# Turning ten column blocks of a weight by DMA in the opening instead of on TensorE between two forward passes

## The chip, the core and the metric

The kernel runs on one core of a Trainium2 chip. Its time is the device time of that core in microseconds (us), from the first to the last instruction and what lies around them; less is better. The times given for it are 2131.66, 2133.43 and 2137.64 us (median 2133.43). The profile is of one more execution.

## The reference, cut to what matters

Four layers, A, B, A, B, each added to the residual stream x (2048 rows of 640, bf16), and the gradients of x and of the four weights. Both layers share the form layer norm, Wqkv, attention over 32 heads of 20, Wo. A is a linear attention, B a softmax attention over a window of 256 rows.

```python
def _A_ref(x, wqkv, wo):
    qkv = ((x @ wqkv).reshape(B, S, 3, H, Dh)).transpose(2, 0, 3, 1, 4)
    q, k, v = qkv[0], qkv[1], qkv[2]
    phi = lambda t: jnp.where(t > 0, t + 1, jnp.exp(t)) + 1e-6
    pq, pk = phi(q), phi(k)
    kv = jnp.einsum("bhsd,bhse->bhde", pk, v)
    z = jnp.einsum("bhsd->bhd", pk)
    num = jnp.einsum("bhqd,bhde->bhqe", pq, kv)
    den = jnp.einsum("bhqd,bhd->bhq", pq, z)[..., None] + 1e-6
    o = num / den
    return o.transpose(0, 2, 1, 3).reshape(B, S, D) @ wo
...
def reference(A_x, A_wqkv, A_wo, B_wqkv, B_wo, B_x, grad_out):
    _const = dict(B_x=B_x)
    def _f(*_d):
        return _fwd_reference(**{'A_x': _d[0], 'A_wqkv': _d[1], 'A_wo': _d[2], 'B_wqkv': _d[3], 'B_wo': _d[4], **_const})
    _out, _vjp = jax.vjp(_f, A_x, A_wqkv, A_wo, B_wqkv, B_wo)
    _grads = _vjp(grad_out)
    _out0 = jnp.asarray(_out)
    return (_out0, *[jnp.asarray(_g) for _g in _grads])
```

The gradient of a product with a weight needs the weight turned (its columns as rows): dx = dy @ W^T. Each weight is turned once, kept in DRAM (WqTA, WoTA, WoTB, WqTB), and read back in the backward phases.

## The kernel before

The 2048 rows are 16 tiles of 128. The forward part has these stretches:

- **The opening** (`a_first(items, 0, 0)`): layer norm of each tile, its transposes on TensorE, Wqkv of the first layer A in six chunks of 320 columns (`a_qkv`), the exponentials on ScalarE, the rest on VectorE. Each tile stores hn (its normed rows, on SP's queue) and pq, pk and v (on ScalarE's queue). The ring of hn has one buffer, so the layer norm of a tile waits until the hn store of the tile before has landed.
- **The first double pass** (`a_kv(0)`, `ab_pass(0, False)`): the sums over the rows of layer A (`a_kv`; L572 are the last "band sums"), then for each tile A's numerator (`a_num`), its projection (`out_proj`), layer B, and the third layer's layer norm and Wqkv.
- **Between the passes** and **the second double pass** (`late_q`, `a_kv(2)`, `turn_w` twice, `ab_pass(2, True)`): the same for layers three and four. The q columns of the third layer are made later (`late_q`, L547), eight tiles of them between the passes.

The backward part follows, phase by phase, with orders of its own. It reads the turned weights back from DRAM long after they were written.

The weights are turned in two ways. `flip_w` lets the DMA turn a block of 128 by 640 of a weight in DRAM into a buffer of the ring KT or e (five and four buffers, which the attention uses later), and stores it to DRAM; it makes twenty flips in the opening, fifteen for B's Wqkv and five for A's Wo, each flip and each store on SP's queue. `turn_w` turns 128 columns with five transposes on TensorE (L906), copies them from PSUM to SBUF on ScalarE (L911), and stores them over SP; it makes the fifteen column blocks of A's Wqkv and the five of B's Wo between the passes. Its three PSUM buffers are the ring `sb`, so every fourth turn waits for the copy of the first. The copies of Wo_B go over the space of v and wait for the last user of it. Operations of `turn_w` and of eight tiles of `late_q` are marked as fillers.

The order of each engine in the forward part comes from a list scheduler, `Sched.order`: it takes the operation that can start first by the durations written with each operation, and a filler counts as starting 300 ns later than it could. A flip or a store of `flip_w` has the kind "B": SP is taken for 1.3 us, and it ends 4.5 us after its start. The items of a stretch are written down in order of a number in tiles (`items`), and a flip additionally waits for the layer norm of a tile (`gate`). Once emitted, each engine works its list in order. SP's and ScalarE's DMAs are counted by eight completion counters that are taken in turn in the order of emission; a DMA waits until the last one of its counter, the eighth before it, has landed.

The lines that the change touches:

```python
for i in range(4 * DT):                       # DT = 5: twenty flips
    at = 4.5 + 0.5 * i
    items.append((at, len(items), flip_w(i, ("rs", 0, int(at) - 1))))
...
turn_w("Wqkv_A", self.QTT, ...)               # QTT = 15 column blocks
turn_w("Wo_B", DT, ...)
```

Of the kernel before, what the change touches and what calls it, by code (L numbers as in the profile page):

```python
# [16 lines left out]
P = 128  # L17
# [69 lines left out]
class Sched:  # L87
# [6 lines left out]
    def op(self, eng, dur, fn, r=(), w=(), dma=None, prio=None, filler=False):  # L94

        o = Op()
        o.filler = filler
        o.eng, o.dur, o.fn, o.dma, o.idx = eng, dur, fn, dma, len(self.ops)
        o.prio = o.idx if prio is None else prio
        o.deps, o.after, o.users, o.bufs, o.est, o.end = set(), set(), [], [], 0.0, None  # L100
        o.start = None
        for k in r:
            if k in self.lw:
                o.deps.add(self.lw[k])
            self.rd.setdefault(k, []).append(o)
        for k in w:
            if k in self.lw:
                o.deps.add(self.lw[k])
            o.deps.update(self.rd.pop(k, ()))
            self.lw[k] = o  # L110
        o.deps.discard(o)
        for k in list(r) + list(w):
            b = k[0] if isinstance(k, tuple) else k
            if isinstance(b, Buf) and b not in o.bufs:
                o.bufs.append(b)
                if b.ops:
                    o.after.add(b.ops[0])
                elif b.idx:
                    o.after.add(b.pool.items[b.idx - 1].ops[0])
                if not b.ops and b.idx >= b.pool.n:  # L120
                    o.deps.update(b.pool.items[b.idx - b.pool.n].ops)
                b.ops.append(o)
        self.ops.append(o)
        return o
# [78 lines left out]
class Kern:  # L203
# [129 lines left out]
    def forward(self, slabs):  # L333
        nc, tc, D, T, TT, DT, H, G, DP = self.nc, self.tc, self.D, self.T, self.TT, self.DT, self.H, self.G, self.DP
# [4 lines left out]
        with ExitStack() as st:  # L339
# [26 lines left out]
            at = [0]  # L366
# [14 lines left out]
            def over_vv(n):  # L381
                vat[0] += n
                assert vat[0] <= TT * D
                return vflat[:, vat[0] - n:vat[0]]
            WoTB = over_vv(DT * D).rearrange("p (k n) -> p k n", k=DT)
# [26 lines left out]
            def dma(eng, out, in_, size, r, w, **kw):  # L412
                def f():
                    with nc.allow_non_contiguous_dma(reason="strided layouts"):
                        dq[eng].dma_start(out=out(), in_=in_())
                op(eng, 60, f, r, w, dma=("D", size), **kw)

            def flip(out, in_, size, r, w, **kw):
                op("SP", 60, lambda: nc.sync.dma_start_transpose(out=out(), in_=in_()), r, w, dma=("T", size), **kw)

            def pe(cols):
                return sum(max(c / 2.4 + 3, 26) for c in cols)

            def av(n):
                return 170 + 0.834 * n
# [463 lines left out]
            def run(items):  # L889
                for _, _, f in sorted(items, key=lambda it: it[:2]):  # L890
                    f()

            def load_w(name, src, eng, k, after=()):
                v = src.rearrange("(kt p) n -> p kt n", p=P)
                dma(eng, lambda: wsb[name][:, k:k + 1, :], lambda: v[:, k:k + 1, :], 2 * P * wsb[name].shape[-1], after, [name])

            def turn_w(name, n, keys, dst, done, after=()):

                F = dict(filler=True)
                for q in range(n):  # L900
                    ps = R["sb"].buf()
                    ps.make = lambda ps=ps: singles[ps.idx % 3].bitcast(BF).rearrange("p (k q) -> p k q", q=P)

                    def f(ps=ps, q=q):
                        for et in range(DT):
                            nc.tensor.transpose(ps.t[:, et, :], wsb[name][:, et, q * P:(q + 1) * P], self.ident)  # L906
                    o = op("PE", pe([P] * DT), f, keys, [ps], **F)
                    o.deps.update(o_ for o_ in R["s3"].items[-1].ops if not o_.filler)
                    turned.append(o)
                    out, key = dst(q)  # L910
                    turned.append(op("ACT", av(D), lambda ps=ps, out=out: nc.scalar.copy(out(), ps.t[:, 0:DT, :]), [ps],  # L911
                                     [key], **F))
                    turned[-1].deps.update(after)
                    turned[-1].deps.discard(turned[-1])
                    done(q, out, key)

            def flip_w(i, gate):
                def f():
                    et, part = divmod(i, 4)
                    src, name, n, a = ((self.B_wqkv, "WqTB", self.QTT, part * DT) if part < 3 else (self.A_wo, "WoTA", DT, 0))  # L920
                    c0 = part * D if part < 3 else 0
                    kind = ("KT", "e")[i % 2]
                    b = R[kind].buf()
                    view = lambda: (b.t if kind == "KT" else b.t.rearrange("p h i q -> p (h i) q"))[:, 0:DT, :]
                    flip(view, lambda: src[et * P:(et + 1) * P, c0:c0 + D], 160 * KB, [gate], [b])
                    S.ops[-1].dma = ("B", 0)
                    dma("SP", lambda: W[name].rearrange("p (a b) -> p a b", a=n)[:, a:a + DT, et * P:(et + 1) * P],
                        view, 160 * KB, [b], [])
                    S.ops[-1].dma = ("B", 0)
                return f  # L930
# [4 lines left out]
            def staged(W_, n):  # L935
                def dst(q):
                    kind = ("KT", "e")[len(turned) // 2 % 2]
                    b = R[kind].buf()
                    return (lambda: b.t[:, 0:DT, :] if kind == "KT" else
                            b.t.rearrange("p h i q -> p (h i) q")[:, 0:DT, :]), b  # L940

                def done(q, out, b):
                    dma("SP", lambda: W[W_].rearrange("p (a b) -> p a b", a=n)[:, q, :].rearrange("p (k q) -> p k q", q=P),
                        out, 160 * KB, [b], [])
                return dst, done
# [103 lines left out]
            items = []  # L1049
# [4 lines left out]
            for i, (k, src) in enumerate((("Wo_A", self.A_wo), ("Wqkv_B", self.B_wqkv), ("Wo_B", self.B_wo))):  # L1054
                for j in range(DT):
                    tt = 1 + 3 * i + j
                    items.append((tt + 0.9, len(items), lambda k=k, src=src, j=j, tt=tt: load_w(k, src, "SP", j, [("vv", tt, 5)])))
            for i in range(4 * DT):
                at = 4.5 + 0.5 * i
                items.append((at, len(items), flip_w(i, ("rs", 0, int(at) - 1))))  # L1060
            run(items)
            a_kv(0)
            ab_pass(0, False)
            for tt in range(EARLY):
                late_q(2, tt, filler=True)
            a_kv(2)
            kv_users = {o for t in range(TT) for k in [("pk", t, 2), ("pk", t, 3), ("vv", t, 4), ("vv", t, 5)]
                        for o in S.rd.get(k, ())}
            turn_w("Wqkv_A", self.QTT, [("Wqkv_A", i) for i in range(6)], *staged("WqTA", self.QTT))
            turn_w("Wo_B", DT, ["Wo_B"], lambda q: (lambda: WoTB[:, q, :].rearrange("p (k q) -> p k q", q=P), ("WoTB", q)),  # L1070
                   lambda q, out, key: None, kv_users)
            R["s3"].items[-1].ops.extend(turned)
            a_users = {o for i in range(6) for o in S.rd.get(("Wqkv_A", i), ())}
# [3 lines left out]
            for rows, kind, size, f in slabs:  # L1077
                keys = [("dOp", t) for t in rows] or [("qkvp", 3, t, i) for t in range(TT) for i in (1, 3, 5)]
# [810 lines left out]
```

## Time and profile before

| | us or share |
|---|---|
| median of three runs | 2133.43 |
| the profiled execution | 2123.76 |
| its span, first to last instruction | 2122.0 |
| TensorE busy | 94% |
| VectorE, ScalarE, GpSimd busy | 69%, 57%, 41% |
| mean granted TensorE clock | 0.981 |
| opening | about 10 to 105 us |
| turns of the weights on TensorE | 386 to 434 us |
| end of the second double pass | about 700 us |

Rows of instructions in order of time read: start, duration, engine, line, operation, tile written and tiles read, and how many are merged in the row. A bracket gives the idle time of the engine ahead of it and what ended that. PE is TensorE, ACT ScalarE, DVE VectorE, POOL GpSimd. SPq and ACTq are the DMA issues of SP and ScalarE; their duration is the time that the issue held the queue, not that of the transfer, which is given as "DMA to landing". Rows of a line read: minimum, median and maximum of the duration in ns, and the first and last start in us.

### The profile page before, as it was taken

The numbers are of one execution on the slowest core, as the hardware profiler recorded it, in microseconds if no ns is written. First come the engines' busy times: TensorE is split into PE (matmuls) and PEld (weight loads), VectorE is DVE, ScalarE is ACT, GpSimd is POOL, SyncE is SP. The second block draws the span as 40 slices with busy tenths as digits, with TensorE's granted clock in tenths as the row PEclk, the third lists the DMA queues.
The fourth block names the chain that finished last, engine by engine and source line by source line (L and its number), as shares of the span: only waits on it lengthen the run. The fifth ranks groups of instructions, "written<-read, shape, count | busy, mean of one in ns | idle before, by whom it ended". The sixth has DMA issues, their size and how long they took to land. (4 is left out here: it accounts for less than half of the span.)

```text
span 2122.0 us, 67891 instructions
## 1 busy us (share of the span) xinstructions
PE 2003.0 (94%) x27908; PEld 1384.9 (65%) x27908; DVE 1456.4 (69%) x3018; ACT 1204.6 (57%) x1995; POOL 878.8 (41%) x1850
## 2 busy tenths in 40 slices
PE   7979999889999899999999899999999999998999
PEld 4746666666666676776666677556777765666764
DVE  7767887677775688999544389407999984445751
ACT  4628888557887588888322133217898881211430
POOL 1026666137777465665232123204666651321210
PEclk9999999999999999999999999998999999999999
DMA  9838988479989688998888999746999989979853
GB/s 283 211 102 185 186 186 179 128 190 198 194 204 184 129 153 153 156 156 169 180 186 184 207 202 210 147 119 132 162 156 160 155 172 177 201 177 228 181 112 101
DMA packets 934471, 365.94 MB, mean 172 GB/s; under 512 B 820752, under 2 KB 914448, under 8 KB 933904
## 3 DMA queue, kind: packets, MB, share of 16 engines
q1 hardware_dynamic: 866176, 299.16, 72.6%
q10 hardware_dynamic: 67984, 62.45, 9.6%
q8 instruction: 218, 3.57, 0.7%
q14 instruction: 93, 0.76, 0.1%
HBM read 109.02 MB, written 101.58 MB: 99 GB/s over the span
## 5 line engine op out<-in xcount | busy, mean ns | idle before, releaser
L1689 DVE TENSOR_TENSOR ds_sb<-pair,e_sb 128x768 bf16<-128x768 f32 x480 | 437.8, 951 | 58.0 <-PE pair L1650 48.6
L1669 ACT ACTIVATE e_sb<-pair 128x768 bf16<-128x768 f32 x480 | 390.8, 815 | 97.2 <-PE pair L1650 68.1
L832 POOL TENSOR_SCALAR_AFFINE_SELECT e_sb<-e_sb 128x384 bf16<-128x384 bf16 (+1 forms) x512 | 197.2, 406 | 334.5 <-ACT e_sb L823 328.0
L823 ACT ACTIVATE e_sb<-s_ps 128x1152 bf16<-128x1152 f32 (+2 forms) x256 | 273.9, 1070 | 93.4 <-PE s_ps L819 66.3
L1681 POOL TENSOR_SCALAR_AFFINE_SELECT e_sb<-e_sb 128x256 bf16<-128x256 bf16 x448 | 182.0, 406 | 228.1 <-ACT e_sb L1669 227.9
L1320 POOL TENSOR_TENSOR gw<-w,gcar 128x640 f32<-128x640 f32 x64 | 89.4, 1397 | 423.3 <-ACT w L1317 402.2
L1131 PEld LDWEIGHTS <-slabR 128*128 128x128 bf16 x1920 | 185.8, 98 | 116.8 <-DMA slabR<-o 6.2
L1678 POOL TENSOR_SCALAR_AFFINE_SELECT e_sb<-e_sb 128x256 bf16<-128x256 bf16 x512 | 206.5, 406 | 90.1 <-ACT e_sb L1669 90.1
L1714 PEld LDWEIGHTS <-dsT 128*128 128x128 bf16 x2880 | 146.4, 97 | 99.0 <-issue 91.8
L1705 ACT COPY dsT<-dsT_ps 128x768 bf16<-128x768 bf16 x240 | 191.2, 796 | 9.5 <-PE dsT_ps L1702 6.6
L447 PE MATMUL mm_ps<-slabR,hnTB 128*128 128x320 bf16 x960 | 166.8, 301 | 4.4 <-DVE oA L647 2.4
L1702 PE MATMUL dsT_ps<-ident,ds_sb 128*128 128x128 bf16 x1848 | 158.9, 224 | 1.2 <-ACT dsT L1705 1.1
L1718 PEld LDWEIGHTS <-e_sb 128*128 128x128 bf16 x2880 | 145.2, 96 | 0.0
L1718 PEld LDWEIGHTS <-ds_sb 128*128 128x128 bf16 x2880 | 145.2, 96 | 0.0
L837 POOL TENSOR_SCALAR_AFFINE_SELECT e_sb<-e_sb 128x512 bf16<-128x512 bf16 x224 | 143.1, 639 | 0.0
L1302 ACT ACTIVATE dh<-mm_ps 128x320 f32<-128x320 f32 x64 | 28.0, 437 | 188.9 <-PE mm_ps L1131 172.8
L1131 PE MATMUL dw_ps<-dqkv,slabR 128*128 128x480 bf16 x640 | 134.5, 366 | 0.0
L1131 PE MATMUL dw_ps<-dqkv,om 128*128 128x480 bf16 x640 | 134.2, 366 | 0.0
L1650 PE MATMUL pair<-slabR 32*128 32x384 bf16 (+2 forms) x1024 | 120.5, 326 | 12.1 <-DVE ds_sb L1689 5.6
L857 PEld LDWEIGHTS <-e_sb 128*128 128x128 bf16 x2880 | 108.3, 96 | 32.6 <-POOL e_sb L837 9.6
L857 PE MATMUL pv_ps<-v_slab,e_sb 128*128 128x32 bf16 x2880 | 121.1, 177 | 6.0 <-POOL e_sb L837 5.2
L1131 PEld LDWEIGHTS <-om 128*128 128x128 bf16 x800 | 77.3, 98 | 71.4 <-DMA om<-o 2.8
(237 smaller groups left out, 4372.6 us busy)
## 6 DMA issues: line engine op xcount, KB each, us to landing
qkvp<-qk_slab SPq DMA_DIRECT2D x64, 256.0 KB, 3.1
hn<-slabR SPq DMA_DIRECT2D x64, 160.0 KB, 3.0
qkvp<-v_slab SPq DMA_DIRECT2D x32, 256.0 KB, 2.7
slabR<-qkvp SPq DMA_DIRECT2D x16, 512.0 KB, 5.4
o<-o SPq DMA_DIRECT2D x48, 160.0 KB, 2.9
pq<-pp ACTq DMA_DIRECT2D x32, 160.0 KB, 2.7
pk<-gcar ACTq DMA_DIRECT2D x32, 160.0 KB, 2.0
v<-vv ACTq DMA_DIRECT2D x32, 160.0 KB, 3.0
```

The source lines that it names most:

```text
L447: nc.tensor.matmul(ps.t[:, w0:w0 + width], lhsT=lhsT(), rhs=rhs(), start=start, stop=stop)
L823: op("ACT", av(3 * nkt * P), lambda: nc.scalar.activation(e.t[:, 0:3, 0:nkt, :], s3.t[:, :, 0:nkt * P].rearrange("p h (i q) -> p h i q", q=P),
L832: nc.gpsimd.affine_select(out=v, in_=v, compare_op=ALU.is_ge, fill=0.0, base=0, pattern=[[0, h1 - h0], [1, P]], channel_multiplier=-1)
L857: nc.tensor.matmul(pv.t[:, h % 16, :], lhsT=e.t[:, hh, j, :], rhs=vts[j].t[:, h, :], start=(j == 0), stop=(j == nkt - 1))
L1131: nc.tensor.matmul(ps.t[:, w0:w0 + width], lhsT=lhsT(), rhs=rhs(), start=start, stop=stop)
L1669: nc.scalar.activation(E[n][:, 2 * p:2 * p + 2], PR[h][:, :, 0:3 * P].rearrange("p i (j q) -> p i j q", q=P), ACT.Exp, scale=self.c_att)
L1678: nc.gpsimd.affine_select(out=e[:, :, j, :], in_=e[:, :, j, :], compare_op=ALU.is_ge, fill=0.0, base=0, pattern=[[0, 2], [-1, P]], channel ...
L1681: nc.gpsimd.affine_select(out=e[:, :, j, :], in_=e[:, :, j, :], compare_op=ALU.is_ge, fill=0.0, base=-1, pattern=[[0, 2], [1, P]], channel ...
L1689: nc.vector.tensor_mul(DS[n][:, hs], PR.pop(h)[:, :, 0:3 * P].rearrange("p i (j q) -> p i j q", q=P), E[n][:, hs])
L1702: nc.tensor.transpose(ps[:, i, j, :], DS[n][:, 2 * p + i, j, :], self.ident)
L1705: (nc.scalar.copy if by == "A" else nc.vector.tensor_copy)(TSB[h], TPS.pop(h))
L1718: nc.tensor.matmul(a[:, 1 + x, hh, :], lhsT=src[n][:, hh, j, :], rhs=ld[g][rhs][:, q, cs], start=(i == 0), stop=(i == len(dkv) - 1))
```

## The change

The ten column blocks of A's Wqkv that belong to q and k are no longer turned by `turn_w`, but by ten more flips behind the twenty; `turn_w` keeps the five of v. Flip 20 and the following take the five row blocks of A's Wqkv in turn, q and k of each, and store them into the first ten parts of WqTA. All thirty flips are spaced by 0.42 of a tile instead of 0.5, and the gate of the last ones is the layer norm of the last tile. The stores of the flips write runs of 128 elements (5 per partition), those of `turn_w` 640 in one run.

```diff
-            def turn_w(name, n, keys, dst, done, after=()):
+            def turn_w(name, qs, keys, dst, done, after=()):
...
-                for q in range(n):
+                for q in qs:
...
             def flip_w(i, gate):
                 def f():
-                    et, part = divmod(i, 4)
-                    src, name, n, a = ((self.B_wqkv, "WqTB", self.QTT, part * DT) if part < 3 else (self.A_wo, "WoTA", DT, 0))
+                    et, part = divmod(i, 4) if i < 4 * DT else ((i - 4 * DT) // 2, i % 2)
+                    src, name, n, a = ((self.A_wo, "WoTA", DT, 0) if part == 3 else
+                                       (self.B_wqkv if i < 4 * DT else self.A_wqkv, "WqTB" if i < 4 * DT else "WqTA",
+                                        self.QTT, part * DT))
                     c0 = part * D if part < 3 else 0
                     kind = ("KT", "e")[i % 2]
...
-            for i in range(4 * DT):
-                at = 4.5 + 0.5 * i
-                items.append((at, len(items), flip_w(i, ("rs", 0, int(at) - 1))))
+            for i in range(6 * DT):
+                at = 4.5 + 0.42 * i
+                items.append((at, len(items), flip_w(i, ("rs", 0, min(int(at) - 1, TT - 1)))))
...
-            turn_w("Wqkv_A", self.QTT, [("Wqkv_A", i) for i in range(6)], *staged("WqTA", self.QTT))
-            turn_w("Wo_B", DT, ["Wo_B"], lambda q: (lambda: WoTB[:, q, :].rearrange("p (k q) -> p k q", q=P), ("WoTB", q)),
+            turn_w("Wqkv_A", range(2 * DT, self.QTT), [("Wqkv_A", i) for i in range(6)], *staged("WqTA", self.QTT))
+            turn_w("Wo_B", range(DT), ["Wo_B"], lambda q: (lambda: WoTB[:, q, :].rearrange("p (k q) -> p k q", q=P), ("WoTB", q)),
```

The scheduler's order of the built programs differs in the opening (SP's list above all), between the passes, and in the first tiles of the second double pass; from its middle on, the lists of all engines are the same again.

## The prediction

> **What bounds the kernel now.** I read the page first, then the busy times of single stretches, then the instructions in order of time where the change takes work away (404 to 445 us) and where it puts work (20 to 110 us).
>
> ```profile
> span 2122.0 us, 67891 instructions
> PE 2003.0 (94%) x27908; PEld 1384.9 (65%) x27908; DVE 1456.4 (69%) x3018; ACT 1204.6 (57%) x1995; POOL 878.8 (41%) x1850
> DMA  9838988479989688998888999746999989979853
> ...
> 36.00:57.00 21.00, 20.16 (x189) 14.78 (x188) 17.61 (x52) 14.03 (x34) 0.00 (x0) 1.00 0.98 255
> 86.00:101.00 15.00, 14.95 (x139) 11.20 (x137) 10.14 (x29) 9.79 (x21) 0.00 (x0) 1.00 0.39 133
> 404.00:445.00 41.00, 34.73 (x369) 25.80 (x366) 31.09 (x88) 16.45 (x33) 0.00 (x0) 1.00 0.71 204
> 500.00:600.00 100.00, 95.93 (x1640) 67.09 (x1644) 73.70 (x186) 79.96 (x122) 73.54 (x153) 1.00 0.92 195
> ```
>
> In a row of a stretch the first pair is its length and TensorE's busy time, and the last three numbers are the granted clock, the DMA engines' busy share and GB/s. TensorE is the bound nearly everywhere: 94% over all, 96% in the second forward pass (500 to 600), full in the opening (20.16 of 21.0 and 14.95 of 15.0). The gap between the forward passes is an exception, 34.73 of 41 us; there the turns stand. The DMA share shows the change's other side: 0.98 in the opening while the twenty flips run, 0.39 once they are through. The flips move to where TensorE has no slack and DMA has little before 80 us and much after.
>
> **What it removes: fifty transposes, ten ScalarE copies and ten stores between the passes.**
>
> ```profile
> L906 PE MATMUL s_ps<-ident,Wqkv_A x75: 216/219/311, 386.0 to 418.6; 128*128 128x128 bf16 x75
> ...
> 406.37 1.00 PE L906 MATMUL s_ps<-ident,Wqkv_A 128*128 128x128 bf16 x15
> 408.80 0.44 PE L906 MATMUL s_ps<-ident,Wqkv_A 128*128 128x128 bf16 x5 [1.43 <-ACT KT L911]
> 409.62 2.11 PE L572 MATMUL mm_ps<-vv,gcar 128*128 128x140 bf16 x32
> 415.54 0.44 PE L906 MATMUL s_ps<-ident,Wqkv_A 128*128 128x128 bf16 x5 [0.90 <-ACT e_sb L911]
> 415.82 1.52 PE L447 MATMUL mm_ps<-slabR,oTA 128*128 128x320 bf16 x10
> 419.64 0.44 PE L906 MATMUL s_ps<-ident,Wo_B 128*128 128x128 bf16 x5 [0.78 <-ACT KT L911]
> 420.55 0.45 PE L463 MATMUL mm_ps<-ident,slabR 128*128 128x128 bf16 x5 [0.20 <-DVE slabR L481]
> 426.74 0.40 PE L463 MATMUL mm_ps<-ident,qk_slab 128*128 128x128 bf16 x4 [0.71 <-DVE qk_slab L688]
> 427.92 1.52 PE L447 MATMUL mm_ps<-slabR,oTA 128*128 128x320 bf16 x10
> 431.41 0.43 PE L547 MATMUL s_ps<-Wqkv_A,pqT 128*128 128x320 bf16 x2 [0.46 <-DVE pp L555]
> 432.64 0.45 PE L463 MATMUL mm_ps<-ident,slabR 128*128 128x128 bf16 x5 [0.80 <-DVE slabR L481]
> ...
> 418.69 0.21 DVE L477 BATCH_NORM_AGGREGATE mv<-st 128x2 f32<-128x12 f32 x1
> 418.89 0.69 ACT L911 COPY KT<-s_ps 128x640 bf16<-128x640 bf16 x1 [0.40 <-PE s_ps L906]
> 419.48 0.30 ACT L478 ACTIVATE rs<-mv,eps_t 128x1 f32<-128x1 f32 x1
> ```
>
> One transpose lasts 219 ns from start to end, but they overlap: fifteen end within 1.00 us and five within 0.44, so ten more take 0.56, or 56 ns each. Fifty are 2.8 us of TensorE. The bracket is the idle time ahead of the row and what ended it: three turns waited 1.43, 0.90 and 0.78 us because the copy of an earlier turn had not freed its bank. That is the upper bound of the gain here, 2.8 + 3.1 = 5.9 us; the lower one is 0, if other waits take the whole of it.
>
> In the changed program the 25 turns of the v columns stay first, and then come three turns of Wo_B ahead of the band sums (L572) and two after them; their copies wait for the last band sum, as in the old program. I walked the first two tiles of the second pass in that order.
> - The band sums are preceded by three turns, not four, and by no wait on a copy: 0.28 and 1.43 us less, against three more matmuls of the late q (0.41, as one chunk of five lasts 0.68) ahead of them. So 1.3 us earlier.
> - The output projection at 415.82 loses the wait of 0.90 ahead of it: 0.9.
> - The layer norm's Ln began at 419.48 although its mean was there at 418.90 (418.69 + 0.21): the copy of a turn held ScalarE. In the new order no copy stands there: 0.5. The second tile has the same pattern at 431: 0.5 again.
> - A group of five turns ahead of tile 0's first Wqkv_B chunk goes: 0.3.
>
> That makes 3.5 us. The count of idle time agrees: before, 1.43 + 0.90 + 0.78 + 0.20 + 0.71 + 0.46 + 0.80 = 5.3 us. After, the turns' waits are gone, but fewer fillers cover the two layer norms. From the projection's end to the next transposes pass 420.55 - (415.82 + 1.52) = 3.2 us and 432.64 - (427.92 + 1.52) = 3.2, 2.7 without ScalarE's delay; seven matmuls of the late q (0.95) stand in each, so 1.75 us stay idle twice, and 0.71 as before, 4.2 in all. 2.8 + 5.3 - 4.2 = 3.9. I take 3.7. The cover that is gone is thus already in the sum: it costs 3.5 us of idle time that was filled. Behind this TensorE is 96% busy, and the order of all engines is the old one again from the middle of the second pass on, so the gain should last to the end.
>
> The page "TensorE: Matmul & The Clock Gate" of the Trainium skill (Part 4: PE-mode transpose) gives about 275 ns for a 128x128 transpose inside a kernel; by that, as an estimate, the fifty would be 13.8 us. The rows above show why it isn't the price here: it is near the 219 ns of one alone, and back to back one costs 56.
>
> **What it adds: ten flips and ten stores in the opening.** All thirty flips are spaced by 0.42 of a tile instead of 0.5, so 2.38 per tile instead of 2.
>
> ```profile
> 42.00 0.44 SPq L415 DMA_DIRECT2D hn<-slabR  x1
> 47.18 0.33 SPq L415 DMA_DIRECT2D hn<-slabR  x1
> 51.49 1.41 SPq L419 DMA_TRANSPOSE e_sb<-in_B_wqkv_dram  x1
> 57.97 0.54 SPq L415 DMA_DIRECT2D hn<-slabR  x1
> 63.76 0.34 SPq L415 DMA_DIRECT2D hn<-slabR  x1
> 89.47 5.44 SPq L415 DMA_DIRECT2D hn<-slabR  x2
> 109.38 0.39 SPq L415 DMA_DIRECT2D mbd<-mbd  x1
> ...
> 56.91 0.33 ACTq L415 DMA_DIRECT2D pq<-pp  x1
> 58.36 0.84 PE L447 MATMUL s_ps<-Wqkv_A,hnTA 128*128 128x320 bf16 x5 [0.70 <-ACT vv L500]
> ...
> L419 SPq DMA_TRANSPOSE KT<-in_B_wqkv_dram x10: 1200/1328/1796, 20.9 to 76.7; - x10
> DMA to landing us min/median/max: 3.3/4.3/6.7
> ...
> L415 SPq DMA_DIRECT2D WqTB<-KT x10: 371/484/1197, 25.4 to 81.8; - x10
> ...
> DMA to landing us min/median/max: 2.9/3.5/4.7
> ...
> DMA to landing us min/median/max: 3.2/3.5/5.3
> ```
>
> The three landing rows are of the twenty flips, of the stores into WqTB and of the hn stores (36 to 79 us). A tile takes 47.18 - 42.00 = 5.18 us. SP is in order, and every flip holds it 1.33 us, every store about 0.5, an hn store 0.34: before, 2 x 1.83 + 0.34 = 4.0 us per tile, after, 2.38 x 1.83 + 0.34 = 4.7, still under 5.18. Behind a flip that waits stands the hn store, whose landing frees hn's one buffer for the next tile's layer norm; with 3.5 us to land it may be 1.7 us late. I walked the new SP order with these medians: the latest hn store ahead of another one is 0.6 to 0.8 us late. Behind the last hn store (94.6, the second of the pair at 89.47) five flips and five stores remain, 5 x 1.83 = 9.2 us; they are through about 107 with their waits, ahead of the mbd store that begins at 109.38 and of the first hn store of the next layer. So SP itself costs nothing, as long as flips stay near 1.33 us.
>
> The tighter limit is another: DMAs of SP and ScalarE take eight completion counters in turn, so each waits until the eighth before it, of either queue, has landed. That is the program's, not the chip's. Per tile there are hn, pq, pk, v, some 0.6 loads of weights, and two DMAs per flip: 8.6 before, 9.4 after. Eight last 8 / 8.6 x 5.18 = 4.8 us before and 4.4 after, against a flip's median of 4.3 and maximum of 6.7. When one is late, ScalarE stands at a store of pq, pk or v, with its exponentials and copies behind it, and then TensorE. The trace has one such case: the pq store of 56.91 follows in its counter the flip issued at 51.49, and 0.7 us of TensorE were lost at 58.36 (the tile took 63.76 - 57.97 = 5.8 us). Seven stores of ScalarE follow a flip in this way in the old order from tile 3 on, ten in the new one; the last of them (v of tile 14, pk of tile 15) come where SP is furthest behind, 1 to 2 us late by my walk. I take 0.3 for three more such chances of 0.7 at the old rate of one in seven, and 1.2 for the last two. Bounds: 0, if the free DMA time after 86 us takes everything, and below that nothing, since no work leaves the opening; above, every one of the twelve tiles from 3 to 14 stretched by 0.9 us, from the one measured stall of 0.7 and what follows, 10.8 us.
>
> The new stores write runs of 128 elements, 256 bytes, where the old ones wrote 1280. The page "DMA: Bandwidth & Descriptors" of the Trainium skill (Specifications) wants 512 bytes for full rate; were each new store twice as slow for it, ten times 3.5 us would be added to the counters' turns. The stores into WqTB have the same short runs, and land in 3.5 us, like hn's with long rows, so the trace bears nothing of this out here.
>
> **Sum.** -3.7 + 1.5 = -2.2 us: the profiled execution would go from 2122.0 to 2119.8 in its span. It ran at 2123.8, below the median 2133.4 of the runs shown; I carry the difference over to that, 2131.2 us.
>
> **Rivals.**
> - **The opening stretches.** If the flips land later than the counters' turn of 4.4 us as a rule, each tile waits and the opening gives 10.8 us instead of 1.5: 2133.4 - 3.7 + 10.8 = 2140.5, slower. For it: the median is at 4.3 now, with DMA at 0.98. Against: of seven chances one was lost, and from 86 us on the share is 0.39. It decides from a median landing of about 4.6 us.
> - **Nothing is gained.** The layer norms and the chain behind them take all that the turns gave up, and the opening costs its 1.5: 2134.9, no change. Against it: the 1.43 us wait lay ahead of the band sums, on that chain.
> - **More is gained.** The turns cost their latency, not their spacing: 50 x 0.219 = 11 us, 2122.5. Against it: the fifteen within 1.00 us. A smaller form is that TensorE waits less in the second pass because copies and stores are gone, up to 5.9 and some 2 us more from its 4% idle: 2125.5.
> - **The change doesn't do what it says**: the scheduler could have put the late q and the turns back into the same places; the built order shows that it didn't. I give it nothing.
>
> **How the numbers follow.** Forecast 0.58, opening stretched 0.18, nothing gained 0.10, more gained 0.14. Within 0.3% (6.4 us) a measurement of this kernel can't tell a change. Of the forecast 0.03 lies under that bound and 0.02 over it; so faster 0.17, same 0.63, slower 0.20. The likeliest case's own range is 2127 (5.9 gained, nothing lost, and a little of noise) to 2136; the range that holds eight of ten goes to 2124, short of the full latency case, and up to 2141, the stretched opening.
>
> **What would show it.** Right: ten flips of in_A_wqkv between 80 and 107 us, no turn of Wqkv_A after 390, the band sums of the second pass about 2 us earlier against the start of the pass, idle of about 1.7 us ahead of the transposes of the first two layer norms, and hn stores still 5.2 us apart up to 95 us. Wrong: tiles of 6 us in the opening with ScalarE's queue standing at pq, pk or v; a mbd store held by a flip; or a second pass that ends where it ended.

## The result

The change made the kernel slower, by 0.33%: median 2139.42 us (2135.57 to 2148.49, 15 runs) against 2131.98 (2129.02 to 2139.66, 15 runs) beside it, ratio 1.0033, 95% interval 1.0021 to 1.0044, which is 4.5 to 9.4 us. A second comparison on another chip (`e8_changed_again` below) gave 1.0011, interval 0.9998 to 1.0023. The forecast was 2131.2 us, 2.2 faster.

**The profile after.** First the page's head and the busy times of single stretches of the changed kernel (columns as before: length, busy time by engine, granted clock, DMA share, GB/s).

```profile
span 2143.5 us, 67777 instructions
PE 2015.7 (94%) x27858; PEld 1388.9 (65%) x27858; DVE 1459.5 (68%) x3018; ACT 1198.8 (56%) x1985; POOL 882.3 (41%) x1850
```

```profile
86.00:101.00 15.00, 13.85 (x130) 10.37 (x128) 9.48 (x28) 9.31 (x21) 0.00 (x0) 1.00 0.97 247
100.00:118.00 18.00, 13.12 (x132) 9.90 (x130) 8.61 (x29) 5.88 (x13) 0.00 (x0) 0.91 0.79 187
414.00:455.00 41.00, 34.90 (x359) 24.54 (x356) 34.12 (x96) 12.10 (x30) 1.54 (x4) 0.98 0.62 174
```

TensorE, full from 86 to 101 us before (14.95 of 15), is busy 13.85 there and 13.12 of 18 up to 118, with DMA at 0.97 instead of 0.39. The granted clock of 0.91 in the second stretch is taken up below. The gap between the passes, ten us later in time, looks as it did. Three starts on TensorE cut the run into pieces: the first num of pass 1, the first score of pass 1, and the first pair matmul of the backward pass. From the order of time, first the kernel before, then the changed one:

```profile
108.86 0.73 PE L447 MATMUL mm_ps<-mbd,pqT 128*128 128x32 bf16 x5 [1.05 <-DVE mbd L613]
133.14 0.23 PE L819 MATMUL s_ps<-QT,KT 32*128 32x128 bf16 x4
710.01 0.57 PE L1650 MATMUL pair<-slabR 32*128 32x128 bf16 x8
```

```profile
117.47 0.73 PE L447 MATMUL mm_ps<-mbd,pqT 128*128 128x32 bf16 x5 [1.05 <-DVE mbd L613]
142.97 0.23 PE L819 MATMUL s_ps<-QT,KT 32*128 32x128 bf16 x4
717.40 0.57 PE L1652 MATMUL pair<-slabR 32*128 32x128 bf16 x8
```

The opening is 8.6 us longer. From the first score to the first pair, which holds both double passes and the turns, it is 574.4 instead of 576.9, 2.4 shorter. The first pair comes 7.4 us late, as much as the medians differ. The profiled execution of the changed kernel loses another 14 us in the backward pass (1426.1 us from the first pair to the end of the span, against 1412.0). Such a difference appears without the change too: a second profile of the kernel before has 1423.6 there (`e14_before_again`), and a second one of the changed kernel 1417.4 (`e8_changed_again`). So the two pieces ahead of it are compared over all profiles below, and the whole by its times.

**The loss in the opening**, in the changed kernel's order of time (SPq and ACTq are DMA issues of SP and ScalarE):

```profile
52.94 0.33 SPq L415 DMA_DIRECT2D hn<-slabR  x1
...
55.74 1.25 SPq L419 DMA_TRANSPOSE e_sb<-in_A_wo_dram  x1
57.04 3.36 SPq L419 DMA_TRANSPOSE KT<-in_B_wqkv_dram  x1
60.50 0.53 SPq L415 DMA_DIRECT2D hn<-slabR  x1
...
65.46 0.34 ACTq L415 DMA_DIRECT2D pk<-gcar  x1
66.18 0.45 PE L463 MATMUL s_ps<-ident,slabR 128*128 128x128 bf16 x5 [1.65 <-DVE slabR L481]
66.40 0.29 ACT L478 ACTIVATE rs<-mv,eps_t 128x1 f32<-128x1 f32 x1 [2.76 <-DVE mv L477]
...
102.83 1.29 SPq L419 DMA_TRANSPOSE KT<-in_A_wqkv_dram  x1
103.38 0.38 ACTq L415 DMA_DIRECT2D pk<-gcar  x1
104.32 0.84 PE L447 MATMUL mm_ps<-Wqkv_A,hnTA 128*128 128x320 bf16 x5
107.53 0.35 ACTq L415 DMA_DIRECT2D v<-vv  x1
107.93 0.44 ACT L515 ACTIVATE ee<-s_ps 128x320 bf16<-128x320 f32 x1 [4.34 <-DMA KT<-in_A_wqkv_dram]
108.42 0.62 PE L447 MATMUL s_ps<-Wqkv_A,hnTA 128*128 128x320 bf16 x3 [3.26 <-ACT ee L515]
...
110.11 1.54 PE L447 MATMUL mm_ps<-Wqkv_A,hnTA 128*128 128x320 bf16 x5
```

At the end of the opening ScalarE stands at the v store of tile 14 until 107.53. The store follows in its counter the flip issued at 102.83, which landed at 107.43; the exponential behind it begins 4.34 us after ScalarE's last work, the profile names that flip's landing, and TensorE stands 3.26 us for the exponential. With 4.6 us to landing this flip was not a slow one: it was issued only about a microsecond before ScalarE came to the store. In the two other profiles of this opening (`e3_flips_and_turns` and `e8_changed_again` below) the same store stands behind the same flip, which landed in 3.5 and 3.4 us there; ScalarE idles 2.71 and 2.21 us, TensorE 1.62 and 1.12. The profile above has a second cost: after the 3.26 us the granted clock was 0.50 from 108.8 to 112.2 us, and five matmuls took 1.54 us that had taken 0.84 at 104.32. In the other two profiles it stayed at 1.00 there.

In the middle an hn store waits on SP behind a pair of flips, one of which holds the queue 3.36 us. DVE waits 2.8 us for its landing at 65.7, because hn has one buffer, and TensorE 1.65 us for DVE. The flip that held the queue, the slowest of all with 8.3 us to landing, holds ScalarE as well: the pk store of tile 7 follows it in its counter and stands until 65.46. The page "Perfetto Trace Analysis" of the Trainium skill (DMA Instruction — HWDGE) says that such a row begins once the semaphores are there and includes the wait for the descriptor generator; by that the 3.36 us are no counter's wait. The trace agrees: the DMA before this flip in its counter had landed 2.5 us before the row begins. What lengthened that issue no run here tells.

**Between the passes** the changed kernel shows what was forecast: the rows of the turns' line, and TensorE's order of time.

```profile
L906 PE MATMUL s_ps<-ident,Wqkv_A x25: 216/219/314, 396.4 to 400.2; 128*128 128x128 bf16 x25
...
417.05 1.00 PE L906 MATMUL s_ps<-ident,Wo_B 128*128 128x128 bf16 x15
419.07 2.11 PE L572 MATMUL mm_ps<-vv,gcar 128*128 128x140 bf16 x32
423.66 0.72 PE L906 MATMUL s_ps<-ident,Wo_B 128*128 128x128 bf16 x10
428.19 0.43 PE L547 MATMUL s_ps<-Wqkv_A,pqT 128*128 128x320 bf16 x2 [1.57 <-DVE pp L555]
428.61 0.45 PE L463 MATMUL mm_ps<-ident,slabR 128*128 128x128 bf16 x5
438.41 0.43 PE L547 MATMUL s_ps<-Wqkv_A,pqT 128*128 128x320 bf16 x2 [1.30 <-DVE pp L555]
439.09 0.45 PE L463 MATMUL mm_ps<-ident,slabR 128*128 128x128 bf16 x5 [0.26 <-DVE slabR L481]
```

Twenty-five turns of Wqkv_A are left and no turn waits. TensorE idles 1.57, and 1.30 + 0.26, ahead of the transposes (L463) of the first two layer norms.

### The profile page after: what moved, and what is told of

The parts are those of the page before. It is cut to its first block, busy times and chain, and to the rows that moved or that the text cites. A ratio compares the mean times of both kernels' runs of the same rounds, so it can differ in the third digit from the quotient of the medians.

```text
span 2143.5 us, 67777 instructions
## 1 busy us (share of the span) xinstructions
PE 2015.7 (94%) x27858; PEld 1388.9 (65%) x27858; DVE 1459.5 (68%) x3018; ACT 1198.8 (56%) x1985; POOL 882.3 (41%) x1850
```

## The experiments

Theory K: flips land late now and then, and through the eight counters that SP and ScalarE take in turn ScalarE stands at its stores of pq, pk and v. Theory H: hn stores on SP come late behind flips, and hn has one buffer. The others: the closer order alone, the ten more flips wherever they stand, their DMA traffic; and for the other side, that the turns were worth nothing. "First num" is the start shown above, "score to pair" the time between the other two. The expected times stand on the 2132 us of the first chip; others ran the kernel before at 2125.9 to 2131.7, so they are read as differences.

| kernel | first num | score to pair | time to before, 95% interval |
|---|---|---|---|
| before | 108.9 | 576.9 | |
| changed | 117.5 | 574.4 | 1.0033, 1.0021 to 1.0044 |
| e1_closer_twenty | 111.5 | 577.3 | 1.0011, 1.0001 to 1.0021 |
| e2_thirty_wide | 113.9 | 574.6 | 1.0003, 0.9990 to 1.0016 |
| e3_flips_and_turns | 116.9 | 576.4 | 1.0029, 1.0016 to 1.0042 |
| e4_turns_off | 110.8 | 572.7 | 0.9999, 0.9986 to 1.0012 |
| e5_two_hn | 122.3 | 573.6 | 1.0049, 1.0033 to 1.0066 |
| e6_held_stores | 112.3 | 574.1 | 0.9993, 0.9977 to 1.0009 |
| e7_gap_flips | 109.5 | 575.3 | 1.0002, 0.9989 to 1.0014 |
| e8_changed_again | 115.4 | 572.7 | 1.0011, 0.9998 to 1.0023 |
| e9_two_hn_same_order | 111.6 | 576.2 | 1.0022, 1.0011 to 1.0033 |
| e10_pool_stores | 109.3 | 571.9 | 0.9996, 0.9981 to 1.0011 |
| e11_held_before | 108.7 | 578.1 | 1.0008, 0.9995 to 1.0021 |
| e12_held_wide | 108.7 | 573.1 | 0.9997, 0.9984 to 1.0011 |
| e13_all_turns_off | 108.6 | 573.3 | 0.9980, 0.9964 to 0.9996 |
| e14_before_again | 109.3 | 576.0 | 0.9997, 0.9982 to 1.0013 |
| e15_pool_wide | 107.4 | 572.2 | 0.9986, 0.9971 to 1.0001 |
| e16_pool_all_flipped | 112.3 | 573.3 | 0.9994, 0.9981 to 1.0007 |

**The same programs again**, for the spread of single profiles.

> The changed kernel once more, for a profile and a time on the chip on which the three others run. By the first comparison 1.0033 of the kernel before, 0.2 to 0.45% slower; first num of pass 1 at 117, within 1.5 us.

> The kernel before once more, for a second profile of its opening and of its forward passes: its first num of pass 1 at 108.9 in the one profile so far, and 109.5, 110.8 and 108.7 in three kernels with the same opening; so 108.5 to 111, ratio 0.999 to 1.001, and from the first score to the first pair 575 to 578.

The six profiles whose opening has the flips of before (before, e4, e7, e13, e14, and e11, which holds eight of ScalarE's stores back) have their first num at 108.6 to 110.8, mean 109.3; the three with the changed opening (changed, e3, e8) at 115.4 to 117.5, mean 116.6. So the opening costs **7.3 us**, where one pair of profiles said 8.6. By the rows that write hn (L481) the two groups are level up to tile 8; the second is 1.5 us later at tile 9, 3.6 at tile 13 and 5.0 at tile 15. The changed kernel itself came out lower than expected, in time (0.11% against 0.2 to 0.45) as in its first num.

**Which part of the change.**

```diff
 e1: the kernel before, twenty flips
-                at = 4.5 + 0.5 * i
+                at = 4.5 + 0.42 * i
 e2: the changed kernel, thirty flips
-                at = 4.5 + 0.42 * i
+                at = 4.5 + 0.5 * i
 e3: the changed kernel
-            turn_w("Wqkv_A", range(2 * DT, self.QTT), ...)
+            turn_w("Wqkv_A", range(self.QTT), ...)
 e4: the changed kernel
-            for i in range(6 * DT):
-                at = 4.5 + 0.42 * i
+            for i in range(4 * DT):
+                at = 4.5 + 0.5 * i
-                    load_w(wq, "WqTA", QTT, "wq")
+                    load_w(wq, "WqTB", QTT, "wq")
```

> The kernel before with its twenty flips 0.42 of a tile apart instead of 0.5; no flips of A's Wqkv, all turns kept. Theory A (how closely the flips stand makes SP and the completion counters late): the stall that the changed kernel shows at 57 to 63 us, among the flips of B, comes back here and the first num of pass 1 starts 3 to 5 us later than the 108.9 of before; about 2135 to 2137. Theory B (the ten more flips at the end of the opening make the cost): the twenty are through earlier and the last tiles have none beside them, so 2132, within 1.5. Theory C (closer order alone costs all of it): 2139 and more.

> The changed kernel with its thirty flips 0.5 of a tile apart, so that some of A's stand behind the last tile's chunks. Theory A: no stall among B's flips, half of the cost of 8.6 us at the first num is gone: 2134 to 2136. Theory B: flips still stand beside the last tiles and ahead of the mbd store, so as the changed kernel, 2138 to 2141. If the closer order is all of it (C): the cost is gone and the gain between the passes is left, 2128 to 2130.

> The changed kernel with the ten turns of A's q and k columns made as well, as before; the q and k blocks of WqTA are written twice with the same values. What the flips cost without what the turns give. If the turns are worth 3 us (from the starts of the two traces): 2142 to 2143, first num of pass 1 at 117 as in the changed kernel. If they are worth nothing, and the opening cost 7.4 in all: 2139 to 2140. If they are worth the 11 us of their latencies: 2150.

> The kernel before with the ten turns of A's q and k columns left out and no flips in their place; the backward pass reads B's turned weights where it read A's, with the same DMAs, so gradients through A's layers come from other weights. What the turns give without what the flips cost. By the sum of the prediction -3.7, by the starts in the two traces -3: 2128 to 2129.5. If the gap's other waits take it: 2132. If the second pass waits less too: 2126 or less.

The closer order alone costs 2.2 us over the mean of 109.3 at the first num and 1.0011 in time, less than theory A expected. Ten more flips in the old spacing cost 4.5 at the first num, the two together 7.3. So each has a part, and neither alone is the cost. They lie in different places: in e1 hn of tile 15 is written at 96.7 us (94.6 is the mean of the six) and the first num follows 14.7 us later, as in before; in e2 it is written at 95.7, and the first num follows 18.2 later, with ScalarE idle for 3.20 us at the v store of tile 14. With the flips but all turns (e3) the time is 1.0029, 6.2 us. Beside the 1.0033 of the changed kernel that is the case of its expectation in which the turns are worth nothing; beside the 1.0011 they are worth 3.8 us, so these times don't settle it.

The turns' worth shows in the score-to-pair column: 576.0 to 578.1 in the five kernels with all turns (before, e1, e3, e11, e14; mean 576.9), 571.9 to 576.2 in the ten without those of q and k and without flips behind the opening (changed, e2, e4 to e6, e8 to e10, e12, e15; mean 573.5): **3.4 us**. In time e4 alone shows 0.2 us less with an interval of -3.0 to +2.6, so it didn't tell 3.4 from nothing.

**Whether that gain reaches the end.** All fifteen turns of A's Wqkv were left out of e4.

```diff
-            turn_w("Wqkv_A", range(2 * DT, self.QTT), [("Wqkv_A", i) for i in range(6)], *staged("WqTA", self.QTT))
```

> The kernel before with all fifteen turns of A's Wqkv left out, those of the v columns too, and no flips in their place; the backward pass reads B's turned weights where it read A's. Leaving out ten shortened the trace up to the end of the forward passes by about 3 us (from the first score of pass 1 to the first pair of the backward pass 572.7 against 576.9) but the time by 0.2, interval -3.0 to +2.6. If what the trace gains reaches the end: 571 or less from score to pair, and 3 to 6 us faster in time (ratio 0.9972 to 0.9986). If the backward pass or the clock gives it back: within 1.5 us of before although the trace is shorter up to the backward pass.

0.9980, that is 4.3 us (0.9 to 7.7), though score to pair is 573.3 and not 571. So what is saved there does come out of the time. How much of the 3.4 of the ten does is only bounded.

**hn's buffer.** Two buffers, first with a newly planned order, then with every engine's order kept.

```diff
 e5
+            R["hn0"] = Ring(2, tiles=R["hnA"].tiles + R["hnB"].tiles, name="hn0")
...
-                        cell["hn"] = R["hnA"].buf()
+                        cell["hn"] = R["hn0" if l == 0 else "hnA"].buf()
 e9
+            two = R["hnA"].tiles + R["hnB"].tiles
+            R["hnA"].get = lambda idx: two[idx % 2] if idx < TT else two[0]
```

> The changed kernel with two buffers for hn in the opening instead of one, the second being the place that the second layer norm of the passes uses later. Theory H (an hn store behind a flip on SP comes late, and the next layer norm waits for its buffer): the waits of DVE for hn (3.2 us in the changed kernel) and the two tiles of 7 to 7.6 us are gone, the first num of pass 1 starts 3 to 5 us earlier than in the changed kernel run beside it, and the time is 3 to 5 us lower. Theory K (the eight counters hold ScalarE's stores behind late flips): the tiles around 57 and 80 us may change, but v and pk of the last tiles are held as before; within 2 us of the changed kernel.

> The changed kernel with every engine's order kept, and two buffers that hn takes in turn in the opening (the run before this with two buffers had a new order of all engines as well). If an hn store that stands behind a pair of flips on SP sets the two stretched tiles (7.6 and 7.0 to 7.9 us in three profiles of the changed order, at 52 to 60 and 75 to 84 us): these two fall to 5.2 to 6 us, the last hn store comes at 95 to 97 instead of 99 to 101, and the time is 2 to 4 us below the changed kernel's, 1.000 to 1.001 of before. If the flips' counters set them too, the tiles stay above 7 us, and 1.001 to 1.003.

e5 was worse than the changed kernel, 1.0049: with the buffer's wait gone the planner drew the first layer norms forward (hn stores at 37.8, 40.2 and 44.0 us), and the first num came at 122.3. It tests another order more than the buffer. In e9, in SP's order of time:

```profile
52.12 0.33 SPq L417 DMA_DIRECT2D hn<-slabR  x1
...
54.91 1.30 SPq L421 DMA_TRANSPOSE e_sb<-in_A_wo_dram  x1
56.26 3.34 SPq L421 DMA_TRANSPOSE KT<-in_B_wqkv_dram  x1
59.70 0.53 SPq L417 DMA_DIRECT2D hn<-slabR  x1
...
62.79 1.40 SPq L417 DMA_DIRECT2D hn<-slabR  x1
```

The hn store is as late as in the changed kernel (59.70 against 60.50), but the next follows 3.1 us later instead of 5.7: the second buffer takes up the delay. DVE's waits for hn, 3.2 us in the changed kernel, are gone, but ScalarE still stands at the pk store of tile 7, until 64.37, and DVE waits 1.65 us for ScalarE instead. The first num, 111.6, is 5.0 earlier than the mean of the changed opening, while the time, 1.0022, lies between the two of the changed kernel; the two tiles stay at 7.6 and 6.9 us, nearer to the second half of the expectation. One profile against a dozen times: how large a part of the cost the buffer has stays open.

**ScalarE's stores held back**, those of pk and v of tiles 12 to 15, in the changed kernel (e6), in the kernel before (e11), and with the flips 0.5 apart (e12). In e6 and e11 ScalarE's list alone differs from that of their base.

```diff
...
+                                put = lambda: dma("ACT", lambda: self.tm_view(sv["v"])[:, tt, :], lambda: vv[:, tt, :], 160 * KB,
+                                                  [("vv", tt, 4), ("vv", tt, 5)] + ["zcol"] * (l == 0 and tt >= 12), [])
+                                held.append(put) if l == 0 and tt >= 12 else put()
... (the same for pk)
             a_kv(0)
+            for put in held:
+                put()
             ab_pass(0, False)
```

> The changed kernel with the stores of pk and v of tiles 12 to 15 issued after the opening's sums instead of in their tiles. Theory K (ScalarE stands at these stores, behind flips in their counters): the wait of 3.3 to 4.3 us at the end of the opening is gone, the mbd store comes 3 to 4 us earlier after the last hn store than in the changed kernel (18.9 us there, from 99.1 to 118.0), and the time is 2 to 4 us lower, less up to 1 us for eight stores at the start of pass 1. Theory H, or the DMA engines being full: the flips stay as late, DVE and TensorE wait elsewhere; within 1.5 us of the changed kernel.

> The kernel before with the stores of pk and v of tiles 12 to 15 issued after the opening's sums. It tells whether holding them helps the changed kernel because of the ten flips or in any case. If because of the flips: as before, within 1.5 us, first num at 109 to 111. If holding them is good by itself: 2 us or more faster than before.

> The thirty flips 0.5 apart and the stores of pk and v of tiles 12 to 15 after the opening's sums: both costs found so far taken away. If these two are all of the cost, first num at 110 to 111.5 and 2 to 3 us faster than before (0.9985 to 0.9992). If the flips behind the last hn store still hold something (the mbd store stands behind them on SP), first num at 113 as with thirty wide alone, and no faster than before.

e6, ScalarE and TensorE in order of time, where the changed kernel had its 4.34 and 3.26:

```profile
102.66 0.43 ACT L502 CAST vv<-s_ps 128x320 bf16<-128x320 f32 x1
103.82 0.84 PE L447 MATMUL mm_ps<-Wqkv_A,hnTA 128*128 128x320 bf16 x5
104.02 0.44 ACT L518 ACTIVATE ee<-s_ps 128x320 bf16<-128x320 f32 x1 [0.93 <-PE s_ps L447]
104.51 0.57 PE L447 MATMUL s_ps<-Wqkv_A,hnTA 128*128 128x320 bf16 x3
...
112.25 0.73 PE L447 MATMUL mm_ps<-mbd,pqT 128*128 128x32 bf16 x5 [1.04 <-DVE mbd L617]
```

ScalarE waits for TensorE now, and TensorE for nobody there. The first num comes at 112.3, 4.4 us earlier than the mean of the changed opening (3.2 earlier than in the profile of the same chip), and 0.9993 stands against 1.0011 of that chip. In the kernel before the same edit leaves the first num at 108.7, within the spread of its profiles, and gives 1.0008, no gain: it is the flips that make these stores dear. With the flips 0.5 apart as well, the first num is back at 108.7, thirty flips or not. The time, 0.9997, doesn't show the expected 2 to 3 us (interval -3.4 to +2.3 us).

**The flips behind the opening**, after the mbd store.

```diff
-            for i in range(6 * DT):
-                at = 4.5 + 0.42 * i
+            for i in range(4 * DT):
+                at = 4.5 + 0.5 * i
...
             a_kv(0)
+            for i in range(4 * DT, 6 * DT):
+                flip_w(i, ("zsel", DT - 1))()
```

> Twenty flips 0.5 apart as before, and A's ten flips behind the opening, after the mbd store, where the DMA share is 0.3 and less; their stores reach into the first tiles of pass 1. If the cost is that the flips stand beside tiles of the opening: first num at 109 to 111 as in the kernel without them, and what the turns give is left: 2 to 3 us faster than before. If the ten flips cost wherever they stand (SP's 18 us, counters taken from pass 1's stores): first score of pass 1 later by 3 us or more, no faster than before.

The opening is as before, and pass 1 starts late. SP's order of time, and from the waits between 108 and 142 us that of DVE for hn (in total, times, longest):

```profile
110.00 0.39 SPq L415 DMA_DIRECT2D mbd<-mbd  x1
110.44 2.01 SPq L419 DMA_TRANSPOSE KT<-in_A_wqkv_dram  x1
...
129.83 1.29 SPq L419 DMA_TRANSPOSE e_sb<-in_A_wqkv_dram  x1
131.17 0.58 SPq L415 DMA_DIRECT2D hn<-slabR  x1
```

```profile
DVE slabR L481 <- DMA hn<-slabR: 4.3, 1, 4.3
```

The hn store of pass 1's first layer norm stands behind all ten flips, at 131.2 us, and the second layer norm waits 4.3 us for the one buffer. From first num to first score it takes 29.7 us (139.17 - 109.47), where before took 24.3 and the other kernels 24.3 to 26.3. Free DMA engines are not enough: SP's queue has to be free too. Here theory H is what happens; the time, 1.0002, is no faster than before.

**ScalarE's stores on a queue of their own.** Stores of pq, pk and v from tile 3 on issued by POOL: in the changed kernel (e10), with flips 0.5 apart (e15), and with the v blocks flipped too (e16, 35 flips). SP's DMAs then have the eight counters to themselves.

```diff
-                                dma("ACT", lambda: self.tm_view(sv["v"])[:, tt, :], ...
+                                dma("POOL" if l == 0 and tt >= 3 else "ACT", lambda: self.tm_view(sv["v"])[:, tt, :], ...
```

> The changed kernel with the stores of pq, pk and v of tiles 3 to 15 of the opening issued by POOL, which has nothing else to do there, instead of ScalarE; same bytes at the same time, a queue of its own. If ScalarE's standing at its stores is the cost of the last tiles, and not the DMA traffic: from the last hn store to the mbd store 14 to 15 us as before (14.8), and the first num of pass 1 at 112 or earlier; the time 2 to 4 us below the changed kernel's. If the traffic is the cost: 116 to 118 as in the changed kernel. POOL's own way of making descriptors may be slower, and pp has two buffers; if that decides, tiles of 6 us and more from tile 3 on.

> Thirty flips 0.5 apart, with the opening's stores of pq, pk and v from tile 3 on issued by POOL. If counters shared with ScalarE were the opening's whole cost and the gain of 3 us lasts: first num at 108.5 to 110, 572 to 574 from the first score to the first pair, 2 to 4 us faster than before (0.9982 to 0.9991). If the traffic of ten more flips still costs: first num above 111 and no faster than before.

> As the changed kernel with POOL's stores (flips 0.42 apart), and the five blocks of A's v columns flipped in the opening too, 35 flips in all; no turn of A's Wqkv is left. Leaving out all fifteen turns gave 4.3 us (0.998). If the opening takes 35 flips as it took 30: first num at 109 to 111 and 3 to 5 us faster than before. If SP or the counters are too full: hn stores over 5.5 us apart from tile 12 on, first num at 113 or later, not faster.

The line of the pq stores in e10 (the duration of the issue in ns, and the landing), and TensorE in order of time; then the same line in the changed kernel (`e8_changed_again`):

```profile
L415 POOL DMA_DIRECT2D pq<-pp x13: 539/539/722, 40.5 to 103.3; - x13
...
DMA to landing us min/median/max: 2.9/4.2/5.4
```

```profile
104.92 2.11 PE L572 MATMUL mm_ps<-vv,gcar 128*128 128x140 bf16 x32
109.32 0.73 PE L447 MATMUL mm_ps<-mbd,pqT 128*128 128x32 bf16 x5 [1.05 <-DVE mbd L613]
```

```profile
L415 ACTq DMA_DIRECT2D pq<-pp x13: 332/333/378, 40.4 to 109.5; - x13
...
DMA to landing us min/median/max: 2.4/3.6/6.1
```

The same thirty flips at 0.42, the same bytes, and the first num at 109.3, as without them: the traffic alone doesn't make the opening long. That ScalarE's place in the counters was all of the 7.3 us is not shown by this run. The planner also put part of the opening in a new order (only e6 is that edit alone), and the kernel before with its stores on POOL was not run: e15's first num, 1.9 us ahead of the mean of before, hints that POOL's stores gain something without the ten flips too. A late hn store costs here as well: DVE waits 2.3 us for one. From the last hn store (97.74) to the mbd store (109.85) it takes 12.1 us. The page "DMA: Bandwidth & Descriptors" of the Trainium skill (Specifications) gives the first byte as some 0.4 us later when GpSimd issues. The pq stores land in 4.2 us, against 3.6 from ScalarE, but SP's hn stores land later in e10 too (4.0 against 3.1), so no run here shows it; nobody waits for the stores of POOL.

e15 has its first num at 107.4, the earliest of all, 572.2 from score to pair, and the lowest time of the kernels that compute the same: 0.9986 of before, 3.0 us, the upper end of the interval at 1.0001. Against the changed kernel's 1.0033 and 1.0011 that is the better version; that it beats the kernel before is likely and not quite proven. With 35 flips (e16) SP is too full: the first num is at 112.3 (113 or later was expected in that case), and at 0.9994, with 1 inside the interval, no gain is shown.

## Why the prediction was wrong

**The sum had two terms, and one was mis-sized.** Measured, -3.4 and +7.3, together +3.9 us; that lies inside the second interval of the change's time (-0.4 to +4.9) and just under the first (4.5 to 9.4). The forecast was -3.7 and +1.5.

- **The turns' gain, -3.7: right.** The band sums of the second pass come 275.3 us after the first score on average in the ten profiles without those turns and 277.3 in the five with them, the 2 us that were forecast (the first pair of profiles alone shows 0.4). The idle ahead of the two layer norms was 1.6 us each against 1.75 forecast, the turns' waits are gone. All turns of Wqkv_A end by 400.2 us, ten later than said, since the whole run is. That it reaches the end was assumed from equal orders; e13 bears it out for fifteen turns.
- **The opening, +1.5: wrong.** "I take 0.3 for three more such chances of 0.7 at the old rate of one in seven, and 1.2 for the last two." Both parts were too small. For the last two the place was right and the size was not: v of tile 14 stood in all three profiles and cost TensorE 3.26, 1.62 and 1.12 us directly, pk of tile 15 in none, and e6 puts pk and v of the last four tiles at 4.4 together. The other 2.9 (112.25 of e6 less 109.3) come from the closer order in the middle, which the old stall rate made 0.3: e1 has 2.2 of it with twenty flips, and with the flips 0.5 apart and the stores held (e12) none is left. The rate itself was wrong. Of the ten stores that follow a flip in their counter, three stand in the changed kernel's trace (pk of tiles 7 and 10, v of tile 14), and two more stand (v of tile 10, pq of tile 11) that follow a flip's own store, a case that the prediction didn't count.
- **The first rival, a stretched opening, came, with 7.3 us of its 10.8, but not by its reason.** Flips did not land later than the counters' turn as a rule (median 4.0 us against 4.4), and not every tile waited. The sign that the prediction named for being wrong, ScalarE's queue standing at pk or v, is what the trace shows.
- **"So SP itself costs nothing, as long as flips stay near 1.33 us": not all of them did.** One issue held SP 3.36 us, and hn stores came 7.6 and 7.0 us apart; the store of tile 8 went out 2.4 us after its rows were written, where the walk had 0.6 to 0.8 for the latest. In e10 two hn stores stand 7.84 us apart (79.58, 87.42), and the first num isn't late, because its other tiles are shorter: from 51.95 to 67.09 us its hn stores are 5.0 us apart, in before 5.4 over the same three tiles.
- **The rival's point of decision, a median landing of 4.6, was wrong too.** The landing of all flips from 20 to 118 us, in the changed kernel and then in e10:

```profile
L419 SPq DMA_TRANSPOSE KT<-in_A_wqkv_dram x5: 1226/1237/1439, 84.2 to 106.1; - x5
...
DMA to landing us min/median/max: 3.2/4.0/8.3
```

```profile
DMA to landing us min/median/max: 3.0/4.6/6.7
```

The median fell from 4.3 to 4.0 while the opening got longer; e10's is 4.6, and its first num is not late. Who is hurt is decided by which instruction follows the flip in its counter, by a slow flip (8.3 us, pk of tile 7), and by a flip of ordinary landing that SP had issued only shortly before (4.6 us, v of tile 14), not by the median.
- **Right beside these:** the ten flips stand at 84.2 to 108.6 us (80 to 107 forecast); the mbd store was held by no flip, it waited for DVE's mbd.
- **The profile's own time.** The forecast was carried from a profiled run at 2123.8 to the median; the spans of single profiles of before differ by 12 us (2122.0 and 2134.3). Differences of 3 us have to be read from starts inside the trace or from many runs.

## What to carry to other kernels

A DMA that is added to a free queue is not free when completion counters are taken in turn by two queues: look up which instruction follows it in its counter, and what compute stands behind that one on its engine; cost it from the time at which its queue can issue it to the slowest landing seen, not by the median landing. Stores that nobody waits for can go late; that gave back 4.4 of the 7.3 us here, and with the flips 0.5 apart all of it. On an idle engine's queue they did as well, though no run shows what that is worth without the ten flips. And moving DMAs to where the DMA engines idle only moves the cost if a store with a single buffer stands behind them on the same queue.

## What the runs showed of the hardware

The issue of a flip held SP 1.2 to 1.5 us mostly, but 3.0 to 3.4 at one and the same place in both profiles of the changed kernel, e3, e6 and e9 (2.5 in e1), behind another flip and a load of 1920 columns; in e10 four flips in a row took 1.23 to 1.28 us each. POOL issued a store in 0.54 us against ScalarE's 0.33. After 3.26 us without a matmul TensorE's granted clock was 0.50 for 3.4 us in the changed kernel, and after 2.11 us in e2 as well; after 1.62 us (e3) and 1.12 us (e8) at the same place it stayed at 1.00.
